# A sliding-window attention with a feed-forward layer: the order of TensorE's work, its PSUM banks and the loads written out as lists, and one more half batch transposed by the crossbar

## The chip, the cores and the metric

The kernel runs on one core of a Trainium2 chip. The metric is the device time of one execution in microseconds (us). The profile comes from one execution; its span runs from its first to its last instruction.

## The reference

```python
def _attn_ref(q, k, v, n_sink, window):          # q, k, v: (4, 8, 768, 64) float32
    scores = scale * np.matmul(q, k.transpose(0, 1, 3, 2))
    keep = (pos[None, :] < n_sink) | ((rel >= 0) & (rel < window))   # n_sink 4, window 128
    scores = np.where(keep, scores, -1000000000.0)
    a = np.exp(scores - np.max(scores, axis=-1, keepdims=True))
    a = a / (np.sum(a, axis=-1, keepdims=True) + 1e-09)
    return np.matmul(a, v)

def _moe_ref(x, w_in, w_out, beta):              # x: (3072, 512), w_in: (512, 2048), w_out: (2048, 512)
    h = x @ w_in
    g = h * (1.0 / (1.0 + np.exp(-beta * h)))
    return g @ w_out                             # (3072, 512) float32
```

The output of the attention, with its heads side by side, is the x of the feed-forward layer.

## The kernel before, in words

The 3072 tokens are cut into eight half batches (hb 0 to 7) of 384 tokens. In each half batch there are four units, one for each pair of heads, so the units run from 0 to 31. All matrix products run in bf16; the float32 inputs are loaded into staging tiles (`q_stage`, `k_stage`, `v_stage`, `wst`) and cast by VectorE (DVE), ScalarE (ACT) or GpSimd (POOL).

The steps of TensorE have letters, and these letters are used throughout:

- **T(u)**, L725: transposes q and k of a unit with an identity, for hb 0 to 2 only; ACT or DVE copies the result from PSUM to `qkT` (L523, L528). From hb 3 on, SyncE issues a crossbar DMA transpose instead (L708).
- **S(n)**, L823: one burst of score products, one, two or three tiles of two PSUM banks each. ACT takes the exponential of a tile (L840), and DVE or POOL set the masked entries to zero (L848, L854, L858). With the last burst of an even half batch, and the first of an odd one, go the scores against the four sink keys (L870, here called F), with an exponential of their own (L874).
- **A(u)**, L926 and, for the sinks, L915: the product with the values. DVE divides by the sums (L930, L932) and leaves `onorm`. In hb 5 and 7 four units are taken together, and the sink products of the four run at the same time on four strips of the array (L899).
- **R(u)**, L952: `onorm` transposed into `xT`, the x of the feed-forward layer. For units 0 to 11 that is three TensorE transposes with an identity and one copy out of PSUM. From unit 12 on (`u >= 4 * CUT`) it is one crossbar DMA transpose, issued by SyncE (L946).
- **H(hb, m)**, L970: one of the 16 up-projections of a half batch: four products of 384 columns, then a tanh on ACT (L975, `t`) and one DVE operation (L977) that makes `g`.
- **O**, L993: a quarter of a down-projection: four products of 512 columns. After four quarters ACT or DVE copies to `osb`, and POOL or, for the last half batch, SyncE issues the store (L1011).
- **Fillers**, L1212: products of `ones` with itself whose result nobody reads, put where TensorE would otherwise have nothing to do in the first part.

Every engine executes a fixed list. The lists are made at build time in two passes. `_program` calls the steps in an order and records every instruction with what it reads and writes. For the start this order is written out by hand (`"T0:63 T1:01 S1:01 ..."`; the digits behind a colon are the PSUM banks). After that a loop (`head`, `choose`, `background`) takes at each point a step that its cost estimates call ready, with a margin of 200 ns, and the bank that comes free first; `background` puts in the loads and the casts. Then `Graph.arrange` goes over the record once more with its own estimates: it may take one of the next few TensorE groups (3, or 10 before 60 us) ahead of the others, chooses the engine of each cast, copy and mask, and places the fillers. `Graph.resolve` turns dependences into semaphore waits.

SyncE issues the loads in the order of its list, the crossbar transposes among them; a wait of one of these holds all behind it. In the start ACT issues the four k loads of hb 0, and SyncE everything else: four q loads, three of v, then q and k of hb 1, beta, and the weights `w_in` (eight loads, L616) and `w_out` (eight).

Of the kernel before, what the change touches and what calls it, by code (L numbers as in the profile page):

```python
# [22 lines left out]
class Op:  # L23
    __slots__ = ("eng", "fn", "deps", "signal", "count", "waits", "sem", "vc", "dma", "seq", "end", "ns", "alts",
                 "group", "tail", "hold", "lock", "chain", "preds", "ready", "left", "succ", "at")


class Graph:
# [6 lines left out]
    HOP = 180  # L35
    SKIP = 3
    PAD = 100
    STRICT = 1
    WIDE, EARLY = 10, 60000
    SLACK = 0  # L40
# [3 lines left out]
    def __init__(self):  # L44
        self.ops = []
        self.writers = {}
        self.readers = {}
        self.last_x = {}
        self.free = {e: 800.0 for e in self.ENGINES}
        self.dma_free = 2500.0  # L50
        self.stalls = [(16000.0, 1100.0), (34000.0, 700.0)]
        self.port = {"gp": 0.0, "dve": 0.0}
        self.group = 0
        self.filler, self.fill_to = None, 0

# [4 lines left out]
    def add(self, eng, fn, ns=0, r=(), w=(), x=(), dma=None, alts=None, after=(), hold=550, chain=None, lock=False):  # L60
# [9 lines left out]
        o.lock = lock  # L70
# [22 lines left out]
        for p, _ in deps:  # L93
            at = max(at, p.end + (0 if p.eng == eng and not p.dma else self.HOP))
# [4 lines left out]
    def fill(self, fn, r):  # L99

        def one():
# [3 lines left out]
            o.signal, o.count, o.waits, o.vc, o.lock = False, 0, [], None, False  # L105
# [3 lines left out]

    def shut(self, o, eng):  # L110

        return self.port["gp" if eng == "dve" else "dve"] if eng == "gp" or eng == "dve" and o.lock else 0.0

    def place(self, o, at):
# [3 lines left out]
        if o.dma:  # L118
# [5 lines left out]
        else:  # L124
            o.end = self.free[o.eng] = at + o.ns

    def at(self, keys):

        t = 0.0
        for k in keys:  # L130
            ws = self.writers.get(k)
            if not ws:
                return None
            t = max([t] + [p.end + self.HOP for p in ws])
        return t

    def bank_at(self, k):
        return max([0.0] + [p.end + self.HOP for p in self.last_x.get(k, ())])

    def arrange(self):  # L140
# [18 lines left out]
        for o in reversed(ops):  # L159
            o.tail = max([s.tail + self.HOP for s in o.succ] + [0.0])  # L160
            if o.eng == "pe":
                o.tail = max(o.tail, after.tail if after else 0.0)
                after = o
            o.tail += o.ns + (2000 if o.dma else 0)
        groups = {}
        for o in ops:
            if o.eng == "pe":
                groups.setdefault(o.group, []).append(o)
        todo_pe = list(groups.values())
        self.free = {e: 800.0 for e in self.ENGINES}  # L170
        self.dma_free = 2500.0
        self.stalls = [(16000.0, 1100.0), (34000.0, 700.0)]
        self.port = {"gp": 0.0, "dve": 0.0}
        new, planned = [], set()

        def ready(o, e):
            return max([0.0] + [p.end + (0 if p.eng == e and not p.dma else self.HOP) for p in o.preds])

        def done(o):
            planned.add(id(o))  # L180
            new.append(o)
            for s in o.succ:
                s.left -= 1
                if s.left == 0 and s.eng != "pe":
                    pool.append(s)
            if id(o) in follow:
                s = follow[id(o)]
                s.left -= 1
                if s.left == 0:
                    pool.append(s)  # L190

        pool = [o for o in ops if o.left == 0 and o.eng != "pe"]
        while todo_pe or pool:
            best = None
            wide = self.SKIP if self.free["pe"] > self.EARLY else self.WIDE
            if todo_pe and todo_pe[0][0].group <= self.fill_to:
                wide = self.STRICT
            for i, grp in enumerate(todo_pe[:wide]):
                own = set(map(id, grp))
                if any(id(p) not in planned and id(p) not in own for o in grp for p in o.preds):  # L200
                    continue
                t, off = self.free["pe"], 0.0
                for o in grp:
                    t = max([t] + [p.end + self.HOP - off for p in o.preds if id(p) not in own and p.eng != "pe"])
                    off += o.ns
                if best is None or t < best[0] - self.SLACK:
                    best = (t, "pe", i)
                if t <= self.free["pe"]:
                    break
            by_eng = {}  # L210
            for o in pool:
                opts = []
                for e, (fn, ns) in o.alts.items():
                    t = max(self.free[e], ready(o, e), self.shut(o, e))
                    if o.dma:
                        t = max(t, self.dma_free - 3000)
                    opts.append((t + ns, t, e))
                _, t, e = min(opts)
                by_eng.setdefault(e, []).append((t, o))
            first = {}  # L220
            for e, c in by_eng.items():
                t0 = min(c, key=lambda x: x[0])[0]
                first[e] = (t0, max((x for x in c if x[0] <= t0), key=lambda x: x[1].tail)[1])
# [4 lines left out]
            for e, (t0, o) in first.items():  # L228
# [4 lines left out]
            if e == "pe":  # L233
                grp = todo_pe.pop(what)
                late = t + self.PAD if t > self.free["pe"] + 40 else t
                self.fill_by = late
                while self.filler and grp[0].group <= self.fill_to and self.free["pe"] + self.filler[0] <= late:
                    o = self.filler[1]()
                    self.place(o, max([self.free["pe"]] + [p.end + self.HOP for p, _ in o.deps]))
# [5 lines left out]
                for o in grp:  # L245
                    self.place(o, max([self.free["pe"]] + [p.end + self.HOP for p in o.preds if p.eng != "pe"]))
# [149 lines left out]
def _program(nc, G, sb, ps, q, k, v, w_in, w_out, beta, out):  # L396
# [4 lines left out]
    CUT = 3  # L401
# [42 lines left out]
    WIDE_W, SPL, BQ = 2, ('act','gp'), "sp"  # L444
# [884 lines left out]
```

## Time and profile before

| what | value |
|---|---|
| times of three executions | 221.48, 222.72, 221.85 us; median 221.85 us |
| span of the profiled execution | 219.7 us; its own time is not recorded apart from the three, so the median stands for it: 2.15 us more than the span |
| TensorE busy | 213.4 us (97%), 1776 products seen |
| DVE, ACT, POOL busy | 138.1, 147.2, 75.2 us |
| fillers (L1212) | 35, 11.3 us |
| start of the first H | 21.17 us |
| granted TensorE clock | 1.000 of full speed |

The page lists busy times by engine, groups of instructions by line, and waits; the timeline gives the start and the length of each instruction. A TensorE product is recorded with its latency, so the records overlap: 40 products of 384 columns are 86.8 / 512 * 40 = 6.8 us by their mean, but take 6.50 us from start to start. Costs are therefore taken here from start to start.

### The profile page before, as it was taken

Reading aid. Unit: us, or ns where it says so; the run is one execution under the profiler, and the core shown is the slowest. Engines: PE = TensorE matmul, PEld = TensorE weight load, DVE = VectorE, ACT = ScalarE, POOL = GpSimd, SP = SyncE. Lnnn points to the kernel's source line nnn. Section 1 sums busy time; section 2 is a strip of 40 time slices with the busy share of each in tenths; the row PEclk is TensorE's granted clock in tenths of the full one; section 3 lists DMA queues with packets and bytes.
Section 4 is the critical chain, followed back from the end, with each engine's and each line's share of the span. In section 5 each row is a group of like instructions: output and inputs, shape, how many; then the busy total and the mean of one; then the engine's idle time right before and its main releaser. Section 6 shows DMA issues by size and latency. Waiting matters only on the chain.

```text
span 219.7 us, 4563 instructions
## 1 busy us (share of the span) xinstructions
PE 213.4 (97%) x1776; PEld 120.8 (55%) x1793; DVE 138.1 (63%) x293; ACT 147.2 (67%) x241; POOL 75.2 (34%) x140
## 2 busy tenths in 40 slices
PE   8999999999999999999999999999999999999995
PEld 3455557555575575446554556446565456465443
DVE  1697899697774278358960788478886248088000
ACT  2698999586975798459865597275886574187211
POOL 7344551112550790067103770184101770100100
PEclk9999999999999999999999999999999999999999
DMA  6999999999989998499837997659949111400122
GB/s 190 240 302 364 357 287 357 371 298 204 226 185 188 225 141 217 92 253 218 196 74 180 228 182 203 139 142 237 136 98 209 40 63 27 144 2 0 51 95 95
DMA packets 94717, 39.86 MB, mean 181 GB/s; under 512 B 82072, under 2 KB 89512, under 8 KB 94696
## 3 DMA queue, kind: packets, MB, share of 16 engines
q1 hardware_dynamic: 91928, 33.28, 68.9%
q0 software_dynamic: 1680, 5.51, 7.5%
q10 hardware_dynamic: 1088, 0.79, 1.1%
q8 instruction: 14, 0.23, 0.5%
q14 instruction: 7, 0.06, 0.1%
HBM read 27.37 MB, written 6.29 MB: 153 GB/s over the span
## 4 chain that ended last, share of the span: by engine, by line
PE 88%; DVE 6%; DMA 3%; ACT 2%; issue 1%; ACTq 0%
PE P L993 38%; PE P L970 36%; PE P L926 5%; PE P L823 4%; DMA k_stage<-in_k_dram 3%; DVE E L858 2%; PE P L725 2%; PE P L952 1%; DVE g L977 1%; PE P L915 1%; DVE E L848 1%; PE P L870 1%; PE P L1212 1%; DVE w_in L528 1%; ACT E L840 0%
## 5 line engine op out<-in xcount | busy, mean ns | idle before, releaser
L970 PE MATMUL P<-xT,w_in 128*128 128x384 bf16 x512 | 86.8, 327 | 0.4 <-ACT w_in L523 0.2
L993 PE MATMUL P<-w_out,g 128*128 128x512 bf16 (+2 forms) x383 | 84.6, 371 | 1.0 <-issue 0.2
L975 ACT ACTIVATE t<-P,hbeta 128x384 f32<-128x384 f32 x128 | 72.4, 590 | 17.6 <-PE P L970 11.0
L977 DVE SCALAR_TENSOR_TENSOR g<-t,P 128x384 bf16<-128x384 f32 x128 | 67.9, 550 | 21.1 <-ACT t L975 15.7
L970 PEld LDWEIGHTS P<-xT,w_in 128*128 128x128 bf16 x512 | 49.0, 98 | 33.4 <-DVE g L977 0.8
L993 PEld LDWEIGHTS P<-w_out,g 128*128 128x128 bf16 x400 | 37.3, 98 | 40.5 <-issue 0.5
L840 ACT ACTIVATE E<-P 128x1024 bf16<-128x1024 f32 x44 | 43.1, 1036 | 14.1 <-PE P L823 14.1
L854 POOL TENSOR_SCALAR_AFFINE_SELECT E<-E 128x512 bf16<-128x512 bf16 x59 | 38.8, 684 | 27.4 <-ACT E L840 27.2
L1011 POOL DMA_DIRECT2D out_dram<-osb x21 | 11.8, 562 | 63.5 <-ACT osb L523 63.5
L523 ACT ACTIVATE osb<-P 128x512 f32<-128x512 f32 x14 | 8.4, 597 | 25.1 <-PE P L993 25.0
L932 DVE TENSOR_TENSOR onorm<-P,rden 128x384 bf16<-128x384 f32 x32 | 17.6, 554 | 0.8
L529 DVE TENSOR_SCALAR osb<-P 128x512 f32<-128x512 f32 x9 | 6.2, 688 | 15.0 <-PE P L993 14.9
L848 DVE TENSOR_TENSOR E<-E,maskS 128x512 bf16<-128x512 bf16 x16 | 8.8, 564 | 10.4 <-ACT E L840 10.4
L926 PE MATMUL P<-vaug,E 128*128 128x65 bf16 x352 | 15.0, 193 | 0.0
L926 PEld LDWEIGHTS P<-vaug,E 128*128 128x128 bf16 x352 | 14.0, 97 | 1.4 <-ACT E L840 0.4
L823 PEld LDWEIGHTS P<-qkT 64*128 64x128 bf16 x288 | 9.5, 94 | 7.6 <-issue 4.3
L823 PE MATMUL P<-qkT 64*128 64x128 bf16 (+1 forms) x288 | 13.2, 230 | 0.1
L1212 PE MATMUL P<-ones 128*128 128x512 bf16 (+1 forms) x35 | 11.3, 446 | 1.1 <-POOL ones L534 1.1
L528 DVE CAST vaug<-v_stage 128x512 bf16<-128x512 f32 x19 | 9.5, 509 | 3.2 <-DMA v_stage<-in_v_dram 3.1
L697 POOL TENSOR_TENSOR kS<-qkT,headm 128x8 bf16<-128x8 bf16 (+1 forms) x10 | 2.5, 251 | 17.7 <-DMA qkT<-k 9.5
L915 PE MATMUL P<-vS,ES 128*128 128x130 bf16 x40 | 8.1, 221 | 0.4 <-DVE vS L682 0.4
L525 POOL TENSOR_SCALAR_AFFINE_SELECT q<-q_stage 128x512 bf16<-128x512 f32 x7 | 4.8, 693 | 10.4 <-DMA q_stage<-in_q_dram 10.4
(64 smaller groups left out, 119.6 us busy)
## 6 DMA issues: line engine op xcount, KB each, us to landing
v_stage<-in_v_dram SPq DMA_DIRECT2D x24, 256.0 KB, 4.8
out_dram<-osb POOLq DMA_DIRECT2D x21, 256.0 KB, 3.6
q_stage<-in_q_dram SPq DMA_DIRECT2D x15, 256.0 KB, 4.8
k_stage<-in_k_dram SPq DMA_DIRECT2D x15, 256.0 KB, 4.9
wst<-in_moe_w_in_dram SPq DMA_DIRECT2D x5, 512.0 KB, 8.3
wst<-in_moe_w_out_dram SPq DMA_DIRECT2D x4, 512.0 KB, 8.1
g<-in_moe_w_out_dram SPq DMA_DIRECT2D x4, 512.0 KB, 6.6
q_stage<-in_q_dram SPq DMA_DIRECT2D x2, 768.0 KB, 7.8
```

The lines of the kernel that those rows point to most:

```text
L528: return lambda e: e.tensor_copy(dst, src)
L823: add("pe", lambda e, dst=dst, kt=kt, kc=kc, rows=rows, q0=q0, nq=nq, u=u: e.matmul(dst, kt[rows, kc:kc + 128], qkT[rows, u % NT, 0, q0:q0 ...
L840: add("act", lambda e, src=src, dst_=dst_: e.activation(dst_, src, AF.Exp, bias=0.0, scale=SCALE), act_ns(1024), w=[("E", z)] + [("m", z, ...
L854: alts = {"gp": (lambda e, dd=dd, sg=sg: e.affine_select(dd, dd, [[0, 4], [sg, 128]], ALU.is_ge, 0.0, base=min(sg, 0), channel_multiplier= ...
L926: e.matmul(A[:, c0:c0 + D + 1], E[t_ % NE][:, i, hh, :], vaug[vz][:, kb % NK, 2 * hp + hh, :], start=a, stop=o, skip_group_check=True), 31,
L932: add("dve", lambda e: e.tensor_tensor(onorm[on][:, :, :, :].rearrange("p m h d -> p (m h) d"), av[:, :, 0:D], rden[on][:, :].unsqueeze(2) ...
L970: add("pe", lambda e, c=c: e.matmul(hp, w_in16[:, c, m * 128:(m + 1) * 128], xT[:, c, t0:t0 + HALF], start=(c == 0), stop=(c == 3)), mm_ns ...
L975: add("act", lambda e: e.activation(tt[ti][:, :], hp, AF.Tanh, bias=0.0, scale=hbeta[:, m:m + 1]), act_ns(HALF) + 93, r=["hbeta"], w=[("t" ...
L977: add("dve", lambda e: e.scalar_tensor_tensor(gt[T_ % NG][:, m, :], tt[ti][:, :], 1.0, hp, ALU.add, ALU.mult), dve_ns(HALF), r=[("t", ti)] ...
L993: add("pe", lambda e, m=m: e.matmul(P[:, bk, 0:n], gt[T_ % NG][:, m, t * 128:(t + 1) * 128], w_out16[:, m, cols], start=(m == 0), stop=(m ...
L1011: add(eng, lambda e: e.dma_start(out_t[3 * T_ + t], osb[z][:, :]), 262144 / 300, r=[("osb", z)], dma=f"do{eng}{z}", hold={"sp": 550, "gp": ...
L1212: G.fill([lambda e, n=n: e.matmul(P[:, 7, 0:128 * n].rearrange("p (a b) -> p a b", a=n), ones[:, :], ones[:, :].unsqueeze(1).to_broadcast( ...
```

## The change

The hand-written start, the loop with its estimates and the bank chooser are gone. In their place stand three strings. `LOADING` is the order of the loads up to the last weight, and the queue of each (`@a` is ACT's). `ORDER` is the whole order of TensorE's steps with their banks; `Z` marks the end of the stretch in which fillers may be placed. `KNOBS` names, for single casts, copies and masks, the engines that may do them and the earliest time (in us of the estimates) at which they may be planned. `arrange` keeps the given TensorE order (it no longer looks ahead), and its estimates of latencies and loads have other numbers. Loads and casts after hb 1, and the crossbar transposes, are still put in by `background`, by what has been done in the order.

Four changes of the work itself come with it: the crossbar is used for R from unit 8 on (`OCUT` is 2, so hb 2 too); A of hb 3 is taken four units together (`QUADS`); k of hb 1 (768 KB), beta, three q loads and two k loads of hb 0 are issued by ACT; and F of hb 0 and 1 is a step of its own (F0, F1) that stands apart from the bursts.

```diff
-    HOP = 180
-    SKIP = 3
+    HOPS = {("act", "dve"): 145, ("act", "pe"): 172, ("act", "gp"): 185, ("dve", "pe"): 147, ("dve", "act"): 140,
+            ("dve", "gp"): 175, ("gp", "pe"): 115, ("gp", "act"): 115, ("gp", "dve"): 115}
+    LATE, LANDED = 205, 30
+    RING, LAG, REACH = 2600, 1150, 1500
+    STALLS = [(5000.0, 750.0), (19000.0, 650.0), (36000.0, 500.0), (41000.0, 800.0)]
...
-            for i, grp in enumerate(todo_pe[:wide]):
-                own = set(map(id, grp))
...
+            if nxt < len(todo_pe) and not open_[todo_pe[nxt][0].group]:
+                best = (starts(todo_pe[nxt]), "pe", None)
...
-    CUT = 3
+    CUT, OCUT = 3, 2
...
-    LANES, QUADS = [6,7], [5,7]
+    QUADS = [3, 5, 7]
...
-        if u >= 4 * CUT:
+        if u >= 4 * OCUT:
             dst = xT[:, hp, t0:t0 + HALF].rearrange("p (m t) -> p m t", m=NK)
             src = onorm[on][:, :, :, :].rearrange("p m h d -> p (m h d)")
             add("sp", lambda e: e.dma_start_transpose(dst, src), 750, r=[("on", on)],
...
-        add("act" if hb == 0 and n == "k" and Q2 else "sp", lambda e: e.dma_start(dst, src), ns, w=keys,
+        add(via or ("act" if hb == 0 and n == "k" else "sp"), lambda e: e.dma_start(dst, src), ns, w=keys,
...
-    for x in "T0:63 T1:01 S1:01 T2:64 T3:46 S0:12 S4:56 S3:34 S2:01 F:2 V:5 A1:1 A0:5 A2:4 R0:5 A3:2 R1:0 R2:4 R3:0".split():
...
-    early = "H0 T4 H1 H2 H3 T5 H4 T6 T7 H5 S5 H6 H7 H8 H9 S6 H10 H11 S7 H12 H13 H14".split()
...
+    LOADING = "q0.0@a k0.2 k0.0@a q0.1@a q0.2@a k0.1 q0.3 k0.3@a b@a k1@a v0.0 v0.2 v0.1 q1 w0 w1 w3 w2 w5 w4 w6 w7 v1.2 v1.0 v1.1 w8 w9 w10 w11 w13 w12 w15 w14"
+    ORDER = "T2:24 T0:62 T1:51 T3:63 S1:45 B:1 F0:1 S0:23 S2:01 S4:45 V:0 S3:23 A0:6 A1:0 A3:1 A2:6 R0:0 T6:32 R1:4 R3:1 Z T7:75 R2:6 T5:03 T4:14 H:5 H:7 H:0 S5:2345 H:6 S6:0123 H:7 H:6 F1:5 H:3 H:4 H:2 H:6 H:4 H:3 H:6 H:5 H:7 A4:4 S7:0123 A5:6 H:4 O:0 O:1 A7:2 O:5 R4:4 A6:6 O O O R6:6 R7:7 R5:3 O O O H:2 H:4 O H:7 O H:4 H:0 O T11:2 T8:6 T9:4 T10:5 H:1 H:0 S8:2345 O:7 H:1 H:6 S9:2345 O H:0 H:5 H:6 H:3 H:0 S10:456 H:1 H:2 O A8:6 O A9:2 O:3 O A10:4 A11:1 O O O:6 S11:0123457 O O O H:7 S12:012345 H:6 H:7 H:0 H:4 H:1 H:2 H:3 H:6 H:4 O:7 H:5 H:1 H:2 H:0 H:6 H:5 O O A12:1032 O O:4 O O O S13:012356 O:7 O S14:01564 O H:3 H:6 H:2 H:1 H:3 O H:1 H:2 A16:7 H:0 H:6 A17:5 H:4 H:3 H:1 O:5 H:0 H:2 H:6 O H:3 A18:6 A19:1 O O O:6 O S15:0123457 O O O:7 H:2 H:4 O O O S16:012345 H:6 H:7 H:0 H:2 H:3 H:6 H:4 H:1 H:0 H:2 H:6 H:3 H:5 O:2 O O H:1 A20:4056 O O:7 O S17:012356 O O O:0 O S18:67124 O O H:3 H:6 H:2 H:4 H:5 H:7 H:1 H:3 A24:0 A25:2 O:4 A26:1 H:2 A27:0 H:5 O H:2 H:7 H:0 H:1 H:3 O H:6 H:5 H:2 H:0 O O:6 S19:0123457 O H:7 O S20:012345 O O:1 O O H:2 O H:4 A28:3620 H:5 H:6 H:4 H:3 H:7 O:1 O H:4 H:0 H:2 O H:7 H:3 H:6 H:4 O O:7 H:0 H:6 H:2 H:5 H:4 O O H:4 O H:0 O:1 H:4 H:7 O H:4 H:2 H:3 O H:4 O O:5 H:0 O O O O:1 O O O O:7 O O O O:3 O O O"
...
+    for x in ORDER.split():
+        x, _, bk = x.partition(":")
+        x, i = x[0], int(x[1:] or 0)
+        forced[:] = [int(c) for c in bk]
+        background()
```

As built, the first TensorE instructions change from ten fillers to seventeen and a half, and the first T from unit 0 to unit 2. Of the four T of hb 1, three stand ahead of the first H in the kernel before, and all four in the changed one. TensorE has 37 fillers instead of 35, 24 instead of 36 R transposes, 28 instead of 40 sink products of single units, and 36 instead of 24 of units taken together. SyncE has 24 instead of 20 crossbar transposes of `onorm`.

## The prediction

> **What bounds the kernel now.** I read the page first, for whether one engine fills the span.
>
> ```profile
> span 219.7 us, 4563 instructions
> ...
> PE 213.4 (97%) x1776; PEld 120.8 (55%) x1793; DVE 138.1 (63%) x293; ACT 147.2 (67%) x241; POOL 75.2 (34%) x140
> ```
>
> TensorE is busy 97%, but 11.3 us of that are fillers. So the second view is TensorE's timeline of the start: when does useful work become dense?
>
> ```profile
> 1.06 4.45 PE L1212 MATMUL P<-ones 128*128 128x512 bf16 x10 [1.06 <-POOL ones L534]
> 5.31 0.53 PE L725 MATMUL P<-ident,q 128*128 128x128 bf16 x3
> ...
> 18.44 0.49 PE L1212 MATMUL P<-ones 128*128 128x512 bf16 x2
> 19.05 0.33 PE L952 MATMUL P<-ident,onorm 128*128 128x128 bf16 x3
> ...
> 21.17 1.46 PE L970 MATMUL P<-xT,w_in 128*128 128x384 bf16 x8 [0.20 <-ACT w_in L523]
> ```
>
> Until 21.17 us TensorE has fillers and little else. The first H waits for ACT's cast of the first weights. From there the chain of waits shows the pitch:
>
> ```profile
> 40.98 0.34 PE P L952 x6
> 41.31 0.86 PE P L993 x4
> 42.18 6.50 PE P L970 x40
> ```
>
> That is 57 ns for a transpose, 215 for a product of 512 columns and 162.5 for one of 384. I added such pitches over all TensorE instructions of the built program from the first H on: 57 for each sink product of a single unit, 29.5 for a value product, 0.11 or 0.055 us for a pair of score products, and about 93 ns for each change between full rows and strips. The sum is 194.4 us. The last O ends streaming at 217.05 (its record ends at 217.26), so the trace has 195.9: only **1.5 us** of waits in the whole dense part. 2.65 us of copy and store follow. Hence 21.17 + 194.4 + 1.5 + 2.65 = 219.7. The table of stretches says where waits remain, and who is near its limit:
>
> ```profile
> 10.50:12.00 1.50, 1.49 (x24) 1.05 (x26) 1.45 (x4) 1.20 (x3) 1.38 (x4) 1.00 0.77 145
> 12.00:14.00 2.00, 1.88 (x24) 0.85 (x19) 1.56 (x4) 2.00 (x3) 0.75 (x4) 1.00 1.08 352
> ...
> 21.20:36.00 14.80, 14.54 (x160) 9.03 (x161) 13.32 (x30) 14.40 (x26) 7.40 (x8) 1.00 1.06 332
> 36.00:52.00 16.00, 15.90 (x118) 9.36 (x117) 14.31 (x33) 11.39 (x20) 1.98 (x3) 1.00 1.04 312
> ...
> 80.00:150.00 70.00, 69.58 (x604) 39.58 (x609) 46.48 (x96) 46.66 (x76) 27.27 (x43) 1.00 0.88 176
> ```
>
> (Columns: stretch, length, busy of TensorE, weight loads, DVE, ACT, POOL, clock, DMA share, GB/s.) Loads run without pause from 12 to 80 us, with one hole at 10.5 to 12. Between 21.2 and 36 ACT is busy 14.40 of 14.80 us. So the change can gain from TensorE work taken away, from 1.5 us of waits, and from the first H.
>
> **TensorE work after the first H.** The pitches are the same; what is added or gone:
> - R of hb 2 by crossbar: 12 transposes * 57 ns = -0.67. Four copies out of PSUM (0.49 each) go too, beside other work, so at nothing.
> - A of hb 3 as four units: 12 sink products at 57 ns are 0.68; four at once they take 135.65 to 135.93 in hb 5, 0.28, and one more change of strips costs 0.09: -0.32.
> - T: all four of hb 1 lie before the first H, not three: 6 * 57 = -0.34 here (it sits in the start instead).
> - F1 alone, and S7 between A4 and A5, add three changes of strips: 3 * 0.093 = +0.28.
>
> Sum -1.05, so 193.35.
>
> **The start.** TensorE's order is fixed, and T2 comes first. Its q chunk is the fourth load on ACT's queue. It is issued at about 2.3 us; the median landing is 5.6 us later for the q loads of the start and 6.6 for k, so between 7.9 and 8.9, and I take 8.3 (an estimate from these two). Cast 0.43 and hand-over give T2 at 8.9, where the first T now starts at 5.31. The seventeen and a half fillers end at about 7.6 (ten take 4.25 us from start to start, those after about 6.5 us take 0.22 each), so they do not hold it. T3 needs the last k chunk and ends at about 11.0, against 10.86. Then ACT's queue, in order, is the chain:
>
> ```profile
> 11.39 2.86 ACT L840 ACTIVATE E<-P 128x1024 bf16<-128x1024 f32 x3
> 14.12 0.30 ACT L874 ACTIVATE ES<-P 128x128 bf16<-128x128 f32 x1
> ...
> 15.21 1.67 ACT L523 ACTIVATE q<-q_stage 128x512 bf16<-128x512 f32 x3
> ...
> 20.40 0.62 ACT L523 ACTIVATE w_in<-wst 128x512 bf16<-128x512 f32 x1
> ```
>
> From 9.3: two copies 0.8, a k cast 0.4, three copies 1.2, and S1 and its hand-over 0.4, so the first exponential at 12.0 (now 9.16). Five exponentials at 0.92 make 4.6, the sink one 0.2 and its wait for F0 about 0.3, a v cast 0.5: 17.6. Then four casts of q and k 2.1, w_in 0.5, four copies 1.5: 21.7 if ACT never waits, 21.3 if S1 overtakes the copies. I take **21.5** for the first H: +0.33 against 21.17. Where the exponentials start earlier today, ACT then stands and waits for tiles; here it is dense, so nearly nothing is lost.
>
> The loads cost nothing on this path. k of hb 1 on ACT's queue runs beside v and fills the hole at 10.5 to 12 (145 instead of 352 GB/s, about 0.9 us), so the weights land about 0.6 to 1.5 us earlier while the first H is no earlier. If that cover were absent, each H at 28 and 31 us would wait about 0.25 as now.
>
> **Waits in the dense part.** 0.7 of the 1.5 us lie between 21 and 36 where H waits for weights or A for v; with the loads ahead of use I let these go and keep **0.8** for the rest. What is late next is ACT: from the first H to the first O it has 16 tanh at 0.49 (four in 2.06 us), six exponentials at 0.92, one sink exponential and a weight cast of 1.0, 14.6 us, against TensorE's 14.0. The O that follow do not need the last tanh, which covers the 0.6.
>
> **The crossbar on SyncE.** The four new transposes stand between two v loads of hb 3 and the loads of hb 4, and wait for DVE's `onorm` of A8 to A11. By the pitches A11 ends near 69, so SyncE goes on at about 70.5, where it now issues these loads from 66.01 on.
>
> ```profile
> L946 SPq DMA_TRANSPOSE xT<-onorm x20: 1202/1258/2202, 85.9 to 187.9; - x20
> ```
>
> Each holds SyncE 1.26 us, 5.0 in all, and lands after 2.4 (the longest 6.4). The last lands at about 72.7; the first H of hb 2 comes at 74.6. Eight loads of about 1.0 and six transposes of 1.3 to 1.7 then bring q and k of hb 4 at about 90; its burst is due at 94.5. Both slacks, 2 and 4 us, hide it; past them it costs one for one.
>
> The Trainium skill (Advanced Engine Details and Errata, X-Bar Transpose) says that trn2's transpose DMAs are as fast as regular ones. The trace has SyncE held 1.26 us by one, and 0.65 by a v load (three in 1.95 us at 91.11); by the rule SyncE would be held 2.4 us less, and the sum would not move.
>
> **The sum.** 21.5 + 193.35 + 0.8 + 2.65 = 218.3. With the 2.15 us that the median lies above the span: **220.4 us**, 0.65% faster. A difference of 0.5%, 1.1 us, is about what can be told from none.
>
> **Rivals.**
> - *The written order gives its saving back as waits* (no change). The present builder leaves 200 ns of margin; the new order has none, e.g. H2.4 takes a bank whose exponential ends, by the rows above, within 0.1 us of its need, and S14 the same. Sixteen bursts after the first H at 0.1 us and the ACT stretch at 0.6 bring waits to 2.5 instead of 0.8: span 220.0, 222.1 us. For it: 14.40 of 14.80 us. Against it: 69.58 of 70 us busy from 80 to 150, in an order just as fixed.
> - *The start becomes a longer chain* (slower). One mechanism: T2 waits for the fourth load on ACT's queue, and TensorE can do nothing else before it. If v on the other queue takes the larger share, that chunk lands 2.5 us later, and each link on ACT with it: first H at 24.0 or more, and as the rest is dense it is paid one for one: span 220.8, 223.0 us from there on, 224 at 25. It decides from a first H at 24.0. Against it: the last ACT chunk now lands by 10.08 at the latest.
> - *SyncE is late* (slower). The four transposes wait for A8 to A11; if loads behind them land 3 us beyond the 4 us of slack, S13 stops TensorE for 3: span 221.3, 223.4 us. The DMA share of 52 to 80 us (1.09) speaks for it, the slack against.
> - A longer idle time of TensorE in the start could lower its clock. The longest now is 0.41 us, and the slow stretch of the first 5.5 us (0.43 instead of 0.22 a filler) would cost up to 2.7 once more. The Trainium skill (TensorE: Matmul & The Clock Gate, Why this matters for your kernels) allows no gaps over about 3 us. By my times the gaps stay under 1.3 us.
>
> **How the numbers follow.** Forecast 0.47; waits instead of work 0.31; long start 0.13; SyncE, clock and the like 0.09. So faster 0.47, same 0.31, slower 0.22. The low end has the first H at 20.5 and 0.2 of waits: 216.7 + 2.15 = 218.8. The high end, 222.9, takes in the rival of waits (222.1) and reaches to where the long start begins; what lies beyond is most of the 0.22.
>
> **What would show it.** First H at 21.3 to 21.9; 24 transposes of L934 in place of 36; first exponential near 12; from 21 to 36 us TensorE busy at least as now; first H of hb 2 without a wait for `xT`; DMA share above 1 at 10.5 to 12. Wrong if the first H starts after 23, if waits from there exceed 2 us, or if TensorE stops before S13.

## The result and the profile after

The changed kernel takes 225.33 us (median of four runs, 224.44 to 225.70) against 221.84 us (four runs) for the kernel before on the same chip: ratio 1.0142, 95% interval 1.0104 to 1.0181. It is slower, by 3.5 us, where 1.4 us faster was forecast. The profiled execution took 225.39 us for a span of 223.7. Of a2_v_act_fill and x3_order_alone below, the profiled run was slow (278.33 us at a granted clock of 0.756, 228.50 us at 0.95), so their profiles are not read and their medians are those of the other runs.

The lines below answer to those shown of before; line numbers are those of the changed kernel (H is L952, O is L975, t is L957, g is L959, the casts of DVE are L520, the crossbar for `onorm` is L928). First the page, with the shares of the chain of work that ended last (SPq is SyncE's queue, ACTq is ACT's):

```profile
span 223.7 us, 4531 instructions
...
PE 216.4 (97%) x1783; PEld 120.1 (54%) x1783; DVE 128.3 (57%) x283; ACT 146.5 (66%) x245; POOL 76.5 (34%) x142
...
PE 58%; DMA 12%; ACT 10%; SPq 10%; DVE 7%; issue 2%; ACTq 1%
```

The same shares of before:

```profile
PE 88%; DVE 6%; DMA 3%; ACT 2%; issue 1%; ACTq 0%
```

TensorE is still "97% busy", with 12.1 us of fillers in it; that number doesn't tell the two kernels apart. The chain does: loads, SyncE's queue and ACT now stand for a third of it, where TensorE stood almost alone. TensorE's timeline of the start, and of the place where it loses most later:

```profile
1.07 6.57 PE L1124 MATMUL P<-ones 128*128 128x512 bf16 x18 [1.07 <-POOL ones L526]
9.78 0.50 PE L716 MATMUL P<-ident,q 128*128 128x128 bf16 x3 [2.14 <-DVE q L520]
...
23.29 2.11 PE L952 MATMUL P<-xT,w_in 128*128 128x384 bf16 x12
...
128.41 6.04 PE L952 MATMUL P<-xT,w_in 128*128 128x384 bf16 x32
134.68 2.21 PE L952 MATMUL P<-xT,w_in 128*128 128x384 bf16 x12 [0.23 <-DVE g L959]
137.34 1.48 PE L952 MATMUL P<-xT,w_in 128*128 128x384 bf16 x8 [0.44 <-DVE g L959]
```

The first T starts at 9.78 after an idle gap of 2.14 us, the first H at 23.29. At 128 us, 32 products take 6.04 us instead of 5.2: small waits for PSUM banks, one after another. And the table of stretches (length; busy of TensorE, weight loads, DVE, ACT, POOL; granted clock; DMA share; GB/s):

```profile
10.50:12.00 1.50, 1.50 (x13) 1.16 (x12) 0.41 (x1) 1.09 (x3) 0.62 (x5) 0.50 1.13 311
12.00:14.00 2.00, 2.00 (x20) 1.42 (x18) 1.26 (x3) 1.36 (x4) 0.36 (x2) 0.69 1.22 267
21.20:36.00 14.80, 14.59 (x133) 8.48 (x130) 13.06 (x29) 14.80 (x29) 7.88 (x10) 1.00 1.00 299
36.00:52.00 16.00, 15.89 (x143) 9.19 (x143) 11.96 (x29) 9.64 (x17) 1.66 (x2) 1.00 1.06 324
80.00:150.00 70.00, 68.97 (x576) 37.06 (x575) 41.96 (x94) 47.00 (x80) 27.58 (x45) 1.00 1.03 185
```

The hole in the loads at 10.5 to 12 is filled (311 instead of 145 GB/s), but the clock there is 0.50. From 80 to 150 TensorE is idle for 1.0 us by this table, where it was 0.4 before, and the DMA share rose from 0.88 to 1.03.

By the prediction's own sum, with its work of TensorE (194.4 before, 193.35 after) and 2.65 us of end in every row, and the waits as what is left:

| | first H | waits | span | median of the runs |
|---|---|---|---|---|
| before | 21.17 | 1.5 | 219.7 | 221.84 |
| forecast | 21.5 | 0.8 | 218.3 | 220.4 |
| after | 23.29 | 4.4 | 223.7 | 225.33 |

Against the forecast, 1.8 us went at the start and 3.6 in the dense part. Of the waits, 2.6 us lie between 100 and 170 us, by the gaps between TensorE's products there; before has none there.

### The profile page after: what moved, and what is told of

Read it like the earlier page. It is cut to its first block, busy times and chain, and to the rows that moved or that the text cites. A ratio compares the mean times of both kernels' runs of the same rounds, so it can differ in the third digit from the quotient of the medians.

```text
span 223.7 us, 4531 instructions
## 1 busy us (share of the span) xinstructions
PE 216.4 (97%) x1783; PEld 120.1 (54%) x1783; DVE 128.3 (57%) x283; ACT 146.5 (66%) x245; POOL 76.5 (34%) x142
## 4 chain that ended last, share of the span: by engine, by line
PE 58%; DMA 12%; ACT 10%; SPq 10%; DVE 7%; issue 2%; ACTq 1%
PE P L975 27%; PE P L952 22%; DMA q_stage<-in_q_dram 6%; SPq L596 5%; SPq L928 5%; ACT E L822 4%; DMA v_stage<-in_v_dram 4%; DVE g L959 4%; PE P L908 3%; ACT t L957 3%; PE P L805 2%; DMA k_stage<-in_k_dram 2%; PE P L716 2%; ACT qkT L515 1%; DVE onorm L914 1%
## 5 line engine op out<-in xcount | busy, mean ns | idle before, releaser
L952 PE MATMUL P<-xT,w_in 128*128 128x384 bf16 x512 | 91.7, 326 | 1.2 <-DVE g L959 0.7
L959 DVE SCALAR_TENSOR_TENSOR g<-t,P 128x384 bf16<-128x384 f32 x128 | 67.2, 550 | 41.9 <-ACT t L957 39.2
L975 PE MATMUL P<-w_out,g 128*128 128x512 bf16 (+2 forms) x400 | 90.7, 371 | 0.0
L957 ACT ACTIVATE t<-P,hbeta 128x384 f32<-128x384 f32 x128 | 70.8, 595 | 28.1 <-PE P L952 22.8
L952 PEld LDWEIGHTS P<-xT,w_in 128*128 128x128 bf16 x512 | 48.1, 98 | 39.0 <-DVE g L959 3.6
L975 PEld LDWEIGHTS P<-w_out,g 128*128 128x128 bf16 x400 | 36.8, 98 | 38.5 <-issue 0.5
L836 POOL TENSOR_SCALAR_AFFINE_SELECT E<-E 128x512 bf16<-128x512 bf16 x60 | 40.7, 698 | 25.3 <-ACT E L822 24.8
L515 ACT ACTIVATE osb<-P 128x512 f32<-128x512 f32 x19 | 11.3, 596 | 21.8 <-PE P L975 21.7
L1124 PE MATMUL P<-ones 128*128 128x512 bf16 (+1 forms) x37 | 12.1, 466 | 1.1 <-POOL ones L526 1.1
L520 DVE CAST q<-q_stage 128x512 bf16<-128x512 f32 (+1 forms) x12 | 6.0, 498 | 12.0 <-DMA q_stage<-in_q_dram 12.0
L830 DVE TENSOR_TENSOR E<-E,maskS 128x512 bf16<-128x512 bf16 x15 | 6.7, 452 | 9.8 <-ACT E L822 9.7
L690 POOL TENSOR_TENSOR kS<-qkT,headm 128x8 bf16<-128x8 bf16 (+1 forms) x10 | 2.0, 209 | 22.5 <-DMA qkT<-k 12.0
L520 DVE CAST vaug<-v_stage 128x512 bf16<-128x512 f32 x12 | 6.0, 498 | 5.8 <-DMA v_stage<-in_v_dram 5.8
L515 ACT ACTIVATE qkT<-P 128x384 bf16<-128x384 bf16 (+1 forms) x11 | 5.6, 567 | 5.3 <-PE P L716 5.3
L912 DVE RECIPROCAL rden<-P 128x6 f32<-128x6 f32 x32 | 5.4, 181 | 3.6 <-PE P L908 3.6
```

The lines of the kernel that those rows point to most:

```text
L515: return lambda e: e.activation(dst, src, AF.Copy, bias=0.0, scale=scale)
L520: return lambda e: e.tensor_copy(dst, src)
L836: alts = {"gp": (lambda e, dd=dd, sg=sg: e.affine_select(dd, dd, [[0, 4], [sg, 128]], ALU.is_ge, 0.0, base=min(sg, 0), channel_multiplier= ...
L952: add("pe", lambda e, c=c: e.matmul(hp, w_in16[:, c, m * 128:(m + 1) * 128], xT[:, c, t0:t0 + HALF], start=(c == 0), stop=(c == 3)), mm_ns ...
L957: add("act", lambda e: e.activation(tt[ti][:, :], hp, AF.Tanh, bias=0.0, scale=hbeta[:, m:m + 1]), act_ns(HALF) + 93, r=["hbeta"], w=[("t" ...
L959: add("dve", lambda e: e.scalar_tensor_tensor(gt[T_ % NG][:, m, :], tt[ti][:, :], 1.0, hp, ALU.add, ALU.mult), dve_ns(HALF), r=[("t", ti)] ...
```

## The experiments

They stand in the order of the argument. The ratio beside a time is to the kernel before on the same chip, whose medians lay between 221.41 and 221.72; medians of different chips are that far apart by themselves. The first four expectations were written before the mechanism was known, and number the theories as they then stood.

### The start

e1_fillers gives the fillers their measured lengths, so that 25 of them reach to the first T and TensorE never stands:

```diff
-    COLD, WARM = 217, 150
+    COLD, WARM = 150, 108
```

> The changed kernel with more fillers (25 instead of 17.5 ahead of the first transposes, and smaller planned sizes after), so that TensorE does not stand idle from 7.64 to 9.78 us. Theory 1, the clock: the idle 2.14 us took the clock down, and 24 transposes at 107 instead of 56 ns cost 1.2 us of the chain to the first exponential. Then the first T stays at 9.8, the first exponential comes at 12.8 instead of 13.96, the first H at 22.1 instead of 23.29, and the time falls by 1.1, to 224.2. Rival, the loads: only the landing of the last q and k chunks sets the chain; then the first exponential stays at 13.9 and the time at 225.3.

Measured: first exponential 12.18 (12.8 expected), first H 21.99 (22.1 expected); the time 226.14 us, ratio 1.0186 (1.0136 to 1.0236): not better at all. In the profiled run, which took 226.77 us, the first H came 1.3 us earlier and the waits after it rose from 4.4 to 7.0 us. What was won at the start was lost again before 160 us.

e2_loads changes the order of the first loads, so that T2's chunk comes first:

```diff
-    LOADING = "q0.0@a k0.2 k0.0@a q0.1@a q0.2@a k0.1 q0.3 k0.3@a b@a k1@a ...
+    LOADING = "q0.2@a k0.2 q0.0@a k0.0 q0.1@a k0.1 q0.3@a k0.3 b@a k1@a ...
```

> The changed kernel with the q and k loads of hb 0 in another order: q of the four units on ACT's queue, k on SyncE's, unit 2 first, the v loads after them. Theory 2, the late chunk: the first T waited for q of unit 2, the fourth load of ACT's queue, which shared the engines with v and landed at 9.28. Then the first T starts near 5.5 us, the first exponential near 11.2, the first H near 20.6 (the exponentials to the first H took 9.3 us in the changed kernel) and the time falls by 2.5, to 222.8. Rival, ACT's chain alone: the copies and casts ahead of the exponentials set it whatever lands first; then the first H stays above 22.5 and the time above 224.5.

Measured: first T at 5.33 instead of 9.78, first exponential 11.00, first H only 22.68, time 228.52, ratio 1.0289 (1.0232 to 1.0346). An earlier first T doesn't even bring an earlier first H in proportion, and the waits became 9.1 us. The expected 20.6 for the first H failed, and the rival (a first H above 22.5, a time above 224.5) was met. Both runs say that something later than the start sets the time.

### The casts that wait for loads

In the profile of after, DVE's timeline shows who stands in front of the `g` that TensorE's banks wait for:

```profile
129.06 0.43 DVE L520 CAST q<-q_stage 128x512 bf16<-128x512 f32 x1 [1.37 <-DMA q_stage<-in_q_dram]
130.91 0.72 DVE L520 CAST q<-q_stage 128x512 bf16<-128x512 f32 x1 [1.42 <-DMA q_stage<-in_q_dram]
131.55 0.54 DVE L959 SCALAR_TENSOR_TENSOR g<-t,P 128x384 bf16<-128x384 f32 x1
133.30 0.86 DVE L520 CAST q<-q_stage 128x512 bf16<-128x512 f32 x1 [1.21 <-DMA q_stage<-in_q_dram]
134.09 1.93 DVE L959 SCALAR_TENSOR_TENSOR g<-t,P 128x384 bf16<-128x384 f32 x4
```

A cast at the head of DVE's list waits for its load, and the `g` behind it wait too; a bank is free only when its `g` is done, so the next H waits. e3_casts names GpSimd for five such casts:

```diff
-    KNOBS = "... m42.0=:175.2 m42.2=:171.8"
+    KNOBS = "... m42.0=:175.2 m42.2=:171.8 cq6.0=g:0 cq6.1=g:0 cq6.2=g:0 cv5.0=g:0 cv5.2=g:0"
```

> The changed kernel with the casts of q of hb 6 and of two v loads of hb 5 on POOL instead of DVE and ACT. Theory 3, casts in the way: between 128 and 137 us DVE's casts waited for loads, the multiplications that free PSUM banks stood behind them in DVE's queue, and TensorE lost 1.75 us. Then these waits go, and the time falls by 1.5 to 1.8, to 223.7. Rival, ACT: twelve H in a row right behind a burst of three exponentials are bound by ACT; then the waits stay and the time stays at 225.3.

Measured: 226.72, ratio 1.0211 (1.0172 to 1.0251). The five casts left DVE (four) and ACT (one), the other lists were planned anew around them, and the same waits came up behind other casts: the longest, 1.66 us at 136.8, stands behind a cast of k on DVE that waits 2.24 us for its load. By the sum the waits are 7.5 us. Moving single casts treats the sign.

Why are the loads late? They are issued by SyncE, whose list in this place was, in after (start, length of the issue):

```profile
107.74 3.32 SPq L701 DMA_TRANSPOSE qkT<-k  x2
111.11 1.26 SPq L701 DMA_TRANSPOSE qkT<-q  x1
112.42 1.26 SPq L701 DMA_TRANSPOSE qkT<-k  x1
113.73 2.58 SPq L701 DMA_TRANSPOSE qkT<-q  x2
116.35 5.88 SPq L928 DMA_TRANSPOSE xT<-onorm  x4
122.27 1.20 SPq L596 DMA_DIRECT2D v_stage<-in_v_dram  x2
123.52 0.63 SPq L596 DMA_DIRECT2D k_stage<-in_k_dram  x1
124.19 2.17 SPq L596 DMA_DIRECT2D q_stage<-in_q_dram  x2
```

Each issue begins within 0.1 us of the end of the one ahead. It is not waiting for an operand, it is full: 9.1 to 9.7 of every 10 us from 70 to 170 us. In before the same place reads:

```profile
111.21 5.15 SPq L946 DMA_TRANSPOSE xT<-onorm  x4
116.41 1.91 SPq L604 DMA_DIRECT2D v_stage<-in_v_dram  x3
```

The v loads start 5.9 us earlier there, while the first H of after is 2.1 us later than that of before. Before uses 9.3 to 9.8 of every 10 us from 40 to 120, but then come two stretches with 8.1 and 8.4 us used.

### The four transposes by themselves

From here on the lists of all engines, as the two builders made them, are kept word for word, and single entries are added, moved or left out; nothing is planned anew. b1_idle_transposes is the kernel **before** with four idle crossbar transposes in SyncE's list, at the place where the change has its own:

```diff
 SyncE's list:
   v loads of hb 3
+  four crossbar transposes of the onorm tiles of hb 2 into a part of xT not yet in use
   k and q loads of hb 4
```

> The kernel before with every engine's list kept as it is, and four idle crossbar transposes added to SyncE's list alone: the onorm tiles of half batch 2 into a part of xT that is not yet in use, behind the v loads of half batch 3 at 69 us; TensorE still makes its own transposes. Theory S: SyncE's list has some 3.5 us unused between 120 and 140 us and little before (9.3 to 9.8 of 10), 5.2 us or more are added at 69, so the loads and transposes of half batches 4 to 6 come 3 to 5 us later, and TensorE waits 0.5 to 2 us more: 222.3 to 223.8. The prediction's reading (SyncE has 4 us of slack at S13 and more later): within 0.3 us of 221.8.

Measured: 225.33 us, ratio 1.0168 (1.0137 to 1.0198). Four transposes that nobody needs, in a stretch in which TensorE had no wait, cost 3.8 us, as much as the whole change and more than either theory expected. SyncE issues them in 5.74 us, and each load and transpose after them comes 3.8 to 5.8 us later, up to the last load at 170.23 instead of 166.23. ACT's timeline shows where it hurts. In before:

```profile
73.40 0.65 ACT L523 ACTIVATE vaug<-v_stage 128x512 bf16<-128x512 f32 x1
73.92 0.65 ACT L523 ACTIVATE k<-k_stage 128x512 bf16<-128x512 f32 x1
75.77 2.85 ACT L840 ACTIVATE E<-P 128x1024 bf16<-128x1024 f32 x3 [1.20 <-PE P L823]
```

In b1:

```profile
73.58 0.66 ACT L453 ACTIVATE vaug<-v_stage 128x512 bf16<-128x512 f32 x1
78.24 0.63 ACT L453 ACTIVATE k<-k_stage 128x512 bf16<-128x512 f32 x1 [4.00 <-DMA k_stage<-in_k_dram]
78.77 1.92 ACT L770 ACTIVATE E<-P 128x1024 bf16<-128x1024 f32 x2
```

A cast of k for hb 4 waits 4.00 us, and behind it in line stand the exponentials of S12, which have nothing to do with hb 4. TensorE answers in its own timeline, and in the clock:

```profile
77.05 0.81 PE L929 MATMUL P<-w_out,g 128*128 128x512 bf16 x3
79.83 0.23 PE L845 MATMUL P<-vS,ES 128*128 128x130 bf16 x1 [1.97 <-ACT E L770]
...
80.48 4.33 PE L906 MATMUL P<-xT,w_in 128*128 128x384 bf16 x16
```

```profile
79.80:82.00 2.20, 2.17 (x20) 1.39 (x21) 2.01 (x6) 2.20 (x3) 2.15 (x4) 0.60 1.37 217
```

1.97 us of idle time, and then 16 products of H in 4.33 us instead of 2.77, at a granted clock of 0.60. Against before, the products of H are 0.2 us late ahead of this place, 2.4 behind the wait, and 4.0 behind the slow stretch, from 84 us to the end. So the whole cost arises here: some 2.2 us by the wait and 1.6 by the clock.

x4_idle_loads has eight idle loads of 96 KB there, instead of the transposes:

```diff
 SyncE's list:
   v loads of hb 3
+  eight loads of 96 KB into parts of xT not yet in use
   k and q loads of hb 4
```

> The kernel before with eight idle loads (96 KB each, into parts of xT not yet in use) at the place in SyncE's list where b1_idle_transposes had its four idle transposes: 8 times 0.58 us of SyncE or more, no crossbar. If any 5 us of work at that place does it: loads of half batch 4 issued 4 to 5 us later, ACT's cast of k waits 3 to 4 us ahead of the exponentials of S12, time 224.3 to 225.5. If it is something that only the crossbar does: 221.6 to 222.5.

Measured: 224.31, ratio 1.0148 (1.0113 to 1.0184), 2.9 us above before; ACT's cast of k waits 3.41 us for its load, and the clock does not drop behind TensorE's wait (1.39 us here). So it is not the crossbar as such: loads do it too, where they put off the loads of hb 4 by some 4 us.

### Is it SyncE's list or the DMA engines behind it?

a1_v_act is the changed kernel with 14 of the 15 late v loads taken from SyncE and put into idle stretches of ACT's list:

```diff
 v loads of hb 3 to 7, all but the first:
-  SyncE's list, issued from 74.3 to 169.9 us
+  ACT's list, in gaps at 68, 91, 95, 113, 118, 121 and 140 us
```

> The changed kernel with every engine's instruction list kept as it is, but 14 of the 15 v loads of half batches 3 to 7 moved from SyncE's list into idle stretches of ACT's list (0.58 to 1.15 us of SyncE each, about 9.3 us in all). Theory S (SyncE's in-order list is full, 96% busy from 40 to 170 us in the changed kernel, so the four added crossbar transposes push every later load back and the casts that wait for those loads hold up t and g behind them on ACT and DVE): the waits of TensorE between 100 and 170 us (2.5 us in the changed kernel's profile) fall below 0.8, DVE's casts wait under 5 us for loads in all (12.6 before), time 222.9 (222.3 to 223.6) if the start is as in the changed kernel's profile. Rival P (the casts are late because DVE and GpSimd get in each other's way, or because the written engine choices and orders are wrong by themselves): the waits stay at 2 us or more and the time at 225.0 to 225.7. Rival A (loads issued by ACT hold up t): slower than 226.

Measured: 226.34, ratio 1.0192 (1.0158 to 1.0227): expected faster, and it is not. SyncE has 14 issues fewer and is hardly earlier, for the others take longer:

```profile
100.45 0.48 SPq L505 DMA_DIRECT2D q_stage<-in_q_dram  x1
100.98 3.87 SPq L505 DMA_DIRECT2D k_stage<-in_k_dram  x2
104.89 1.13 SPq L505 DMA_DIRECT2D q_stage<-in_q_dram  x1
```

Two k loads hold it 3.87 us, where after has 1.75 (101.42 to 103.17). DVE's casts now wait much less (q 0.5 instead of 4.7 us, v 0.0 instead of 5.8), but TensorE waits for `xT`. Its transposes land up to 7.7 us after their issue where the v loads run from the other queue (6.5 to 7.7 at 68 to 74 us; in after 2.8 to 4.4):

```profile
104.59 0.66 PE L861 MATMUL P<-xT,w_in 128*128 128x384 bf16 x3 [1.07 <-DMA xT<-onorm]
```

Between 70 and 135 us TensorE waits 3.2 us for `xT` and never for a `g`, which comes behind t. So the rival that loads issued by ACT hold up t, whose time (above 226) was met, is not what happened. The DMA share from 40 to 170 us is 0.99 here, 0.96 in after. Another queue was no relief here; that the engines behind the queues are full is the likely reason, and this run doesn't test it by itself.

a2_v_act_fill adds e1's fillers to it.

> The same moves of the v loads, and the longer fillers of e1_fillers (25 ahead of the first transposes). Theory S: e1's first H at 22.0 stays and its waits after 60 us (5.4) fall to about 1: 21.99 + 193.35 + 1.6 + 2.65 = 219.6 of span, 221.7 of time (221.0 to 222.6), against 226.1 for e1. Rival P: within 1 us of e1, 225 to 227.

Measured: 224.42 (five runs, 224.33 to 226.45), ratio 1.0160 (1.0117 to 1.0203); outside the 221.0 to 222.6 of the theory, like a1.

x1_no_late_v leaves those 15 v loads out altogether: no issue, no bytes.

```diff
 SyncE's list:
-  15 v loads of hb 3 to 7
```

> The changed kernel with every list kept, but the 15 v loads of half batches 3 to 7 left out altogether (their casts read what an earlier half batch left in v_stage, so the result differs): neither SyncE nor the DMA engines carry them. Theory S2 (the chain of loads and crossbar transposes, SyncE's list and the DMA engines behind it together, is full from 40 to 170 us and sets TensorE's pace; moving the v loads to ACT's list in a1_v_act left the DMA engines as full): the last q/k transpose of half batch 4 is issued by 91 (92.6 in the changed kernel), that of half batch 7 by 162 (169.2), TensorE's waits between 100 and 170 us fall from 2.5 to under 0.8, time 222.9 (222.2 to 223.6). Rival P (the written places of the casts and engine choices are wrong by themselves): 224.8 to 225.7, waits still 2 us.

Measured: 222.46, ratio 1.0056 (1.0028 to 1.0084). By the medians 2.9 us are gone, by the distances from before on each chip 2.4 (3.5 and 1.1), as the theory of the full chain had it. By the profiles the waits fell from 4.4 to 1.8 us. Its own marks were met in part: TensorE's gaps from 100 to 170 us fell from 2.6 us to nothing, but SyncE was done with the transposes of q and k of hb 4 and 7 at 92.1 and 166.0 us, not at 91 and 162. In the dense part DVE's casts no longer wait for q or v. For v that follows from the edit, as the casts have no load to wait for; for q (4.7 us in after, 0.0 here) it is the chain. How the gain divides between the two isn't shown. The table of stretches, 40 to 170 us, of x1:

```profile
40.00:170.00 130.00, 128.95 (x1107) 73.59 (x1123) 81.53 (x180) 90.50 (x151) 49.29 (x79) 1.00 0.79 166
```

and of after:

```profile
40.00:170.00 130.00, 128.91 (x1093) 71.59 (x1092) 79.22 (x177) 87.95 (x147) 48.03 (x78) 1.00 0.96 193
```

and of before:

```profile
40.00:170.00 130.00, 129.27 (x1097) 74.37 (x1105) 90.50 (x188) 92.47 (x151) 46.79 (x76) 1.00 0.95 191
```

TensorE's busy time does not tell the three apart. The DMA share tells x1 from after, 0.79 against 0.96, but not after from before, which carries as much (0.95) without such waits. The share shows how little room is left; whether TensorE waits depends on how late each load is for its use.

x2_no_late_v_fill is x1 with e1's fillers.

> x1_no_late_v with the longer fillers of e1_fillers. Theory S2: with the chain out of the way the earlier start counts at last: first H at 22.0, waits 1.5, 221.6 (220.8 to 222.4), against 226.1 for e1_fillers. Rival P: 225 to 227.

Measured: 221.92, ratio 1.0031 (1.0005 to 1.0057), against 226.14 for the same fillers with the loads in. But for the 15 loads, the order of the lists of SyncE, ACT, DVE and GpSimd is the same in the two, so it is by the loads that waits of 7.0 us become 1.7. But the first H lies at 23.32, not at the expected 22.0 (x1: 23.17). So this run doesn't show what an earlier start is worth with the loads out of the way; that the time came within the expected 220.8 to 222.4 is luck in this respect. Even with 15 loads left out, the changed order isn't faster than before.

### The order without the crossbar

e4_no_crossbar has the changed order, with R of hb 2 on TensorE again:

```diff
-    CUT, OCUT = 3, 2
+    CUT, OCUT = 3, 3
...
-A8:6 O A9:2 O:3 O A10:4 A11:1 O O O:6 S11
+A8:6 O A9:2 O:3 O R8:0 A10:4 A11:1 O R9:5 O R10:7 R11:0 O:6 S11
```

> The changed kernel with R of hb 2 on TensorE again (four groups of three transposes put into the order ahead of the fourth burst of hb 3). Theory 4, the crossbar saves what it takes off TensorE: time up by 0.7, to 226.0. Rival: the four transposes on SyncE hold the loads behind them until A11 is done, and these come too late for the casts of hb 4; then undoing it gives the loads back earlier and the time falls below 225.3 by up to 1.

Measured: 226.07, ratio 1.0190 (1.0144 to 1.0237), the number of theory 4, but by luck: a gain and a loss cancel. Its loads are in time: SyncE is done with the transposes of q and k of hb 4 and 7 at 89.8 and 159.5 us (after: 92.6 and 169.2), and there is no wait at all from 100 to 150. It loses elsewhere: first H at 22.90, and one place on DVE:

```profile
82.48 1.03 DVE L959 SCALAR_TENSOR_TENSOR g<-t,P 128x384 bf16<-128x384 f32 x2
83.43 2.00 DVE L520 CAST k<-k_stage 128x512 bf16<-128x512 f32 x1
85.35 1.00 DVE L959 SCALAR_TENSOR_TENSOR g<-t,P 128x384 bf16<-128x384 f32 x2
```

A cast that takes 0.41 us elsewhere took 2.00, in a stretch in which GpSimd worked without pause (83.31 to 85.52). Six `g` stood behind it, and TensorE waited 1.72 us. Against after, e4's products of H are 0.5 us early at 63 us, 0.2 late at 77 (the transposes), 2.1 late behind this wait and up to 101 us, and 0.2 early again at 153: with its loads in time, e4 wins 2.3 us between 101 and 153, where after waits. x3_order_alone puts this cast behind three of them and adds e1's fillers:

```diff
 DVE's list:
-  cast of k4.2, g(2,4), g(2,5), g(2,6), ...
+  g(2,4), g(2,5), g(2,6), cast of k4.2, ...
```

> e4_no_crossbar (the written order, half batch 2 transposed by TensorE) with the longer fillers of e1_fillers, and the one DVE cast that took 2.00 us at 83.4 while GpSimd worked, with six g multiplications queued behind it, put behind three of these. Its q/k transposes were not late (issued by 89.8 and 159.5). If the start (22.9) and that one wait (1.87) are all that e4_no_crossbar lost beside the crossbar: first H 22.0, 226.1 - 0.9 - 1.7 = 223.5 (222.6 to 224.4). If waits of the written order turn up elsewhere as they did in e1_fillers: 225 to 226.

Measured: 223.22 (three runs, 223.13 to 224.57), ratio 1.0119 (1.0074 to 1.0163). The time agrees with the forecast of 223.5 from single causes; without a profile to read, the causes themselves aren't shown. It is still some 2 us above before, and where is open.

### Could the lists have been arranged around the late loads?

c1_casts_later takes b1 (before, with the four idle transposes) and moves all 36 casts of hb 4 to 7 back by 4.4 us in the lists of ACT, DVE and GpSimd, so that they stand in front of nothing.

```diff
 lists of ACT, DVE, GpSimd:
-  casts of hb 4 to 7 where before has them
+  each behind everything that started in the 4.4 us after it
```

> b1_idle_transposes (the kernel before with four idle crossbar transposes in SyncE's list at 69 us, every later load some 4.4 us later), with all 36 casts of half batches 4 to 7 moved 4.4 us further back in the lists of ACT, DVE and GpSimd, behind the exponentials, t, g and masks that they had held up. If what cost 3.8 us in b1_idle_transposes is that the casts stand in line ahead of that work (ACT's cast of k waited 4.00 us ahead of the exponentials of S12): TensorE's wait at 78 (1.97) and the slow stretch behind it go, 221.7 to 222.8. If it is that the loads and transposes themselves come too late for TensorE, whatever stands where: 224.5 to 226, with the waits moved to S13 at 94 us.

Measured: 225.96, ratio 1.0229 (1.0163 to 1.0296), no better. But the profile divides the question. The wait at 78 us is gone, and S13, which needs q and k of hb 4, starts its exponentials at 94.93 instead of 94.57 in before (the products of H are 0.36 us late from 67 us on): q and k have the slack that the prediction gave them. TensorE then stops at A16 instead:

```profile
104.41 0.36 PE L856 MATMUL P<-vaug,E 128*128 128x65 bf16 x6 [1.02 <-DVE vaug L458]
...
105.67 0.45 PE L856 MATMUL P<-vaug,E 128*128 128x65 bf16 x9 [0.81 <-DVE vaug L458]
```

and DVE says why, in its timeline:

```profile
102.72 0.88 DVE L600 TENSOR_TENSOR vS<-vS,own 128x512 bf16<-128x512 f32 x1 [3.73 <-DMA vS<-in_v_dram]
103.53 0.41 DVE L778 TENSOR_TENSOR E<-E,maskS 128x512 bf16<-128x512 bf16 x1
103.86 0.49 DVE L458 CAST vaug<-v_stage 128x512 bf16<-128x512 f32 x1
```

The load of the first values (`vS`) stands in SyncE's list behind the transposes of q, k and `onorm` and is as late as these. The operation on `vS`, which was not moved, waits 3.73 us for it (in before it has no wait), and the masks and casts that A16 needs stand behind it. The v loads themselves landed between 100.00 and 102.37, before A16's turn at 103.39. The second wait above has the run itself as its cause: the moved cast starts at 105.19, behind two `g`. So has a third, 1.18 us at 152.7, for a cast of v on GpSimd: the loads of v had landed by 148.04, and it now stands behind three masks. So this run shows that an operation in line ahead of others is the mechanism here too, and that 4.4 us for all casts alike is no cure. Whether a better arrangement could hide the late loads stays open.

## Why the prediction was wrong

**Right.** TensorE's work: by the sum above, with 193.35 us, x1 is left with 1.8 us of waits at its own first H, against 1.5 before, so little can be missing from that term. The hole in the loads is filled. The first H of hb 2 had no wait for `xT`, and S13 did not stop for late q and k. From 21.2 to 36 us "TensorE busy at least as now" held (14.59 of 14.80 us, 14.54 before; the first 2 us are now still the start), and ACT is now busy 14.80 of 14.80. The profiled execution took 1.7 us more than its span, not 2.15. Two of its own signs of being wrong came: a first H after 23, and waits above 2 us.

**Wrong: "Both slacks, 2 and 4 us, hide it."** This is the step that decides. I followed the four transposes to the first H of hb 2 and to S13 and stopped there. Three consumers were left out. The casts, which stand in line on ACT and DVE ahead of work that is already due (4.00 us of waiting in b1); the `vS` load of hb 4, which stands behind the transposes and whose operation held DVE for 3.73 us (c1); and everything after hb 4, since a list that is used 9.3 to 9.8 of 10 us gives only part of a delay back (5.8 us behind the four transposes in b1, still 4.0 at the last load). I had read SyncE's timeline at one place; and the DMA share of 0.88 from 80 to 150 is a mean that hides stretches of 1.01 (100 to 110) and 1.48 (120 to 130). The price I put at nothing is 3.8 us where the lists were planned without the transposes (b1), 1.6 of it by the clock behind the wait. In the changed kernel, whose plan knows of them, taking 15 loads off the same chain brings 2.4 to 2.9 us (x1), and taking the four transposes out, with all lists planned anew, 2.3 us between 101 and 153 us (e4). Their price with its lists kept was not measured.

**A rival had the right cause, the wrong place and the wrong price.** "SyncE is late" was named, at S13, past 4 us of slack, and shared 0.09 with the clock and the like. The v loads in after start 5.9 us later than in before at 122, and this is paid at the casts of hb 5 and 6; S13 did not wait.

**Wrong: the first H at 21.5.** It lies at 23.29 in after and between 21.87 and 23.32 in the profiles of kernels with the same first loads, so the term was short by 0.4 to 1.8, and by 1.8 in after. Two links: T2's chunk landed at 9.28, not 8.3, and the idle gap before it, which I had put under 1.3 us, was 2.14 and took the clock to 0.50. Without the drop of the clock (x2) the first exponential comes at 12.04, as forecast, and the first H still at 23.32: DVE's cast of k of hb 1, whose load now goes by ACT's queue and lands at 14.04, waits 1.69 us with masks and sums behind it. So "the loads cost nothing on this path" was false. How much of the rest this wait costs isn't shown: in e1 it is 1.09 us, and the first H comes at 21.99. What the start's 1.8 us cost in the end is open too, as e1 won 1.3 of them and lost them again in waits while the loads were late.

**The rival of waits**, which had the largest share of the three, was wrong in price (2.5 us of waits, where 4.4 came) and in mechanism: not many small misses of planned times, but mostly casts that wait for late loads.

**The price of a transpose.** I had set it beside that of a load, and the two idle runs tell them apart: four transposes of 96 KB put off the loads behind them by some 4.4 us (b1), eight loads of 96 KB by some 4.0 (x4), which is 1.1 us a transpose against 0.5 us a load of the same size. The rule of the Trainium skill (Advanced Engine Details and Errata, X-Bar Transpose), as fast as regular transfers, is not what these runs show.

## What to carry to other kernels

A queue with no visible wait can be full. Before adding issues to it, look at its own timeline for gaps, and at the DMA share by stretches of ten microseconds rather than seventy: where issue follows issue, whatever is added is a delay of everything behind it, to the end of the stretch. A high share alone says nothing of waits: before had 0.95 from 40 to 170 us and hardly a wait. Follow the delay to every consumer in line, above all to the casts that stand at the head of an in-order engine, and test it by adding the same work idle to the old kernel: four entries in one list told here what a rewritten program did not. And an earlier start was worth nothing here while the loads set the pace (e1).

## What the runs showed of the hardware

- **The clock after a short idle gap.** Idle gaps of TensorE of 1.96 us (x1), 1.97 (b1) and 2.14 (after) were each followed by 3.4 us at a granted clock of 0.50 by the trace (0.60 and 0.69 above are means over stretches that reach past it). Gaps of 1.57 (a1), 1.72 (e4), 2.26 (e3) and 2.77 (e4, in the start) were not followed by any drop. So between 1.5 and 3 us it isn't the length alone that decides. The Trainium skill (TensorE: Matmul & The Clock Gate, Why this matters for your kernels) puts the limit at gaps of about 3 us; here gaps of 2 us were enough, though not each time.
- **Another queue was no relief.** With 14 loads moved to ACT's queue, two k loads on SyncE's took 3.87 us to issue instead of 1.75, and the `xT` transposes issued from 68 to 74 us landed after 6.5 to 7.7 us instead of 2.8 to 4.4 (a1).
- **A DVE cast beside GpSimd.** Casts of 128x512 took 0.41 us and, in a stretch in which GpSimd was busy without pause, 2.00 us (e4). That the one comes from the other isn't shown.
